# Batch 0 of a retention-plus-experts kernel, regrouped by token halves, with zero matmuls ahead and the remainder taken up later

## The chip, the cores and the metric

The kernel runs on one core of one Trainium2 chip. A core has TensorE (PE in the profile; its weight loads are PEld), VectorE (DVE), ScalarE (ACT), GpSimd (POOL) and SyncE (SP), each with its own instruction queue that is worked off in order, and 16 DMA engines that all queues share. The metric is the device time of one execution in microseconds (us); lower is better. Eight runs of the kernel before have a median of 561.19 us and lie between 557.19 and 563.51 us.

## The reference

Two layers follow one another. The first is a retention layer (attention with a decay per head and no softmax), the second mixes four small networks ("experts") with weights given per token.

```
q, k, v: [8 batches, 8 heads, 576 tokens, 64]
scores = q @ k.T / 8
ret    = scores * gamma[h] ** (i - j)      for i >= j, else 0      gamma[h] = 1 - 2 ** (-5 - h)
attn   = ret @ v                           -> x: [4608 tokens, 512]
p      = domain_probs / sum(domain_probs)  [4608, 4]
out    = sum over e of p[:, e] * (relu(x @ w1[e]) @ w2[e])     w1: [4, 512, 1024], w2: [4, 1024, 512]
```

## The kernel before

**Tokens and tiles.** The 4608 tokens are worked in 9 tiles of 512, `t = 0..8`. A batch has 576 tokens, so tile 0 is the first 512 tokens of batch 0, and tile 1 begins with the last 64 tokens of batch 0. `xt[t]` holds the attention output of a tile, transposed, as four blocks of 128 features (two heads each) by 512 tokens. The up projection multiplies it with `w1[e]` into PSUM, a relu writes it to `h`, and the down projection multiplies `h` with `w2[e]`.

**Attention in pieces.** The first 512 tokens of batches 0 and 1 are cut in four `Unit`s each, `(hf, g)`: the half `hf` of 256 tokens and the group `g` of four heads. For a unit, `cast` scales k by a decay table and turns k, q, v to bf16 (k on VectorE, q on ScalarE, v on GpSimd or ScalarE). A transposition of q and k follows: for batch 0 on TensorE (`trans_pe`, L477, with copies out of PSUM on ScalarE, L485, and on VectorE, L486), for batch 1 by a DMA on SP's queue (`trans_dma`, L488). `scores` multiplies k by q and VectorE masks the result (L508). `kv` makes the running key-value state, which ScalarE copies to `sbd` (L538). `values` adds both shares, and VectorE writes them to `xt` times the table `gq` (L570). Units of `hf = 1` also need the state of `hf = 0`. The last 64 tokens of a batch are the remainder, `Rem`: `cast` (L290, L293), two DMA transpositions into `kT` and `qT` (L299), `scores` (L305), `values` (L311, L313) for all heads at once.

**The start.** SP issues the loads of the four units of batch 0 (12 loads of 256 KB, L117), then those of the mixing weights. ScalarE makes the four tables `gq` (L157) before the first cast. Then the units run in the order (0,0), (1,0), (0,1), (1,1), as the loop at L587 writes them. GpSimd issues the weight loads in this order: `w1[0]` between two casts, `w2[0]`, `w1[1]`, `w2[1]`, `w1[2]`, the remainder of batch 0, `w2[2]`, unit 0 of batch 1, `w1[3]`, unit 1 of batch 1, `w2[3]`. Each weight load writes 1 MB as bf16 from fp32.

**Tile 0 and its slots.** For each of the four experts the loop at L691 issues four `up_group`s (8 matmuls of 512 columns each) and two `down_plain`s (16 matmuls of 512 columns each). After each of these six pieces `run(slots, n)` issues what was put into the slot of that number, so slot 6e+i is after up group i of expert e, and slots 6e+4 and 6e+5 are after the down pieces. The order of the instructions is written out by hand; each engine takes its own in this order. In the slots of tile 0 lie:

- the remainder of batch 0: `cast` and the DMA transpositions at 11, `scores` at 15, `values` at 16
- the four units of batch 1 (vs[0] to vs[3]): cast and DMA transpositions at 14, 17, 21, 24; scores and kv at 18, 21, 24, 28; values at 19, 22, 26, 30 (24 and more are slots of tile 1)
- four loads of the mixing weights of tile 1, `pB`, 256 KB each, on SP, at 17
- sums of w2 blocks on VectorE (`w_sum`) from 17 on

Tiles 1 to 8 follow with the same kind of slots. Their down projection uses seven products in place of eight.

**PSUM.** All matmul results go through a ring of four tiles of two banks (`ring_tile`), so a piece can only start when the reader of the piece four before it is done. In tile 0 the reader of an up piece is the relu on ScalarE (L330).

Of the kernel before, what the change touches and what calls it, by code (L numbers as in the profile page):

```python
# [9 lines left out]
FP32 = mybir.dt.float32  # L10
BF16 = mybir.dt.bfloat16
Copy = mybir.ActivationFunctionType.Copy
Exp = mybir.ActivationFunctionType.Exp
Relu = mybir.ActivationFunctionType.Relu
MULT = mybir.AluOpType.mult
# [8 lines left out]
def kernel(  # L24
# [10 lines left out]
    nc = tc.nc  # L35
    B, H, S, D = q.shape
    N, E = moe_domain_probs.shape
    _, Dm, F = moe_w1.shape
# [3 lines left out]
    NC = 4  # L42
    SM = NC * C
    R = S - SM
    NP = H // 2
    NDC = Dm // 128
    NFC = F // 128
    NT = 512
# [7 lines left out]
    const = ctx.enter_context(tc.tile_pool(name="const", bufs=1))  # L56
# [5 lines left out]
    tpool = ctx.enter_context(tc.tile_pool(name="tpool", bufs=1))  # L62
# [3 lines left out]
    def ring_tile(name, shape, dt=FP32):  # L66
        return ring.tile(shape, dt, tag="ring", name=name)
# [19 lines left out]
    rawr = {n: const.tile([128, NP, 2, D], FP32, name=f"rawr_{n}") for n, _ in srcs}  # L87
# [11 lines left out]
    def load_w1(e):  # L99
        return nc.gpsimd.dma_start(out=w1_sb[e], in_=moe_w1[e].rearrange("(dc p) f -> p dc f", p=128))  # L100
# [7 lines left out]
    epool = early.enter_context(tc.tile_pool(name="epool", bufs=1))  # L108


    NU = 4
# [6 lines left out]
                          in_=src[b, 4 * g:4 * g + 4, 2 * C * hf:2 * C * hf + 2 * C, :]  # L118
                          .rearrange("h (p r) d -> p h (r d)", r=2))

    units0 = ((0, 0), (1, 0), (0, 1), (1, 1))
    p0 = epool.tile([128, NT // 128, E], FP32, name="p0")
    prb = tpool.tile([128, N // 128, E], FP32, tag="p1", name="prb")
    for u, (hf, g) in enumerate(units0):
        load_unit({n: raw0[u][n][:, :, :, :].rearrange("p h r d -> p h (r d)") for n in "kqv"}, 0, hf, g, nc.sync)
    nc.sync.dma_start(out=p0, in_=moe_domain_probs[0:NT, :].rearrange("(g p) e -> p g e", p=128))
    nc.sync.dma_start(out=prb, in_=moe_domain_probs.rearrange("(p t) e -> p t e", p=128))


    pos_0 = epool.tile([128, 2, 2], FP32)  # L130
    nc.gpsimd.iota(pos_0, pattern=[[2 * C, 2], [1, 2]], base=0, channel_multiplier=2,
# [14 lines left out]
    for h in range(H):  # L146
        nc.vector.tensor_scalar_mul(gk0[:, :, h, :], pos_0, -lg[h])
    nc.scalar.activation(gk0, gk0, Exp)
    lgp = epool.tile([128, NP], FP32)
    for p in range(NP):  # L150
        nc.vector.memset(lgp[0:64, p:p + 1], lg[2 * p])
        nc.vector.memset(lgp[64:128, p:p + 1], lg[2 * p + 1])
    lsc = epool.tile([128, 1], FP32)
    nc.vector.memset(lsc, math.log(scale))
    gq = const.tile([128, NP, S], FP32)
    for p in range(NP):
        nc.scalar.activation(gq[:, p, :], pos_i, Exp, scale=lgp[:, p:p + 1], bias=lsc)  # L157

    tri = const.tile([128, C], BF16)
# [4 lines left out]
    def later_constants():  # L164
        nc.gpsimd.memset(tri, 1.0)
        nc.gpsimd.affine_select(out=tri, in_=tri, compare_op=mybir.AluOpType.is_ge, fill=0.0,
                                base=0, channel_multiplier=-1, pattern=[[1, C]])
        nc.gpsimd.tensor_copy(trir[0:R], tri[0:R, 0:R])
        nc.gpsimd.tensor_copy(trir[R:2 * R], tri[R:2 * R, R:2 * R])
        pos_j = epool.tile([128, NC + 1], FP32)  # L170
        nc.gpsimd.iota(pos_j[:, 0:NC], pattern=[[C, NC]], base=0, channel_multiplier=1,
                       allow_small_or_imprecise_dtypes=True)
        for j in range(2):
            nc.gpsimd.iota(pos_j[64 * j:64 * j + 64, NC:NC + 1], pattern=[[0, 1]], base=SM, channel_multiplier=1,
                           allow_small_or_imprecise_dtypes=True)
        for h in range(H):
            nc.vector.tensor_scalar_mul(gk[:, :, h], pos_j[:, 0:NC], -lg[h])
        nc.scalar.activation(gk, gk, Exp)
        nc.vector.tensor_scalar(gkr, lgp, pos_j[:, NC:NC + 1], -1.0, op0=MULT, op1=MULT)
        nc.scalar.activation(gkr, gkr, Exp)  # L180
        for n in "kqv":
            nc.gpsimd.memset(rawr[n], 0.0)


    NTT = N // 128
# [1 line left out]
    pn, psm = pns[:, 0:E, :], pns[:, E, :]  # L187
    pd = dpool.tile([E, N], FP32, name="pd")

    ps0 = epool.tile([128, NT // 128], FP32, name="ps0")  # L190
    pm0 = const.tile([128, NT // 128, E], FP32, name="pm0")

    def mixing_weights0():
        nc.vector.tensor_reduce(ps0, p0, axis=mybir.AxisListType.X, op=ADD)
        nc.vector.tensor_scalar_add(ps0, ps0, 1e-9)
        nc.vector.reciprocal(ps0, ps0)
        nc.vector.tensor_tensor(pm0, p0, ps0[:, :].unsqueeze(2).to_broadcast([128, NT // 128, E]), op=MULT)

    def mixing_weights():
        nc.vector.tensor_reduce(psm, prb, axis=mybir.AxisListType.X, op=ADD)  # L200
        nc.vector.tensor_scalar_add(psm, psm, 1e-9)
        nc.vector.reciprocal(psm, psm)
        nc.vector.tensor_tensor(pn, prb[:, :, :].rearrange("p t e -> p e t"),
                                psm.unsqueeze(1).to_broadcast([128, E, NTT]), op=MULT)
        nc.sync.dma_start(out=pd[:, :].rearrange("e (p t) -> p e t", p=128), in_=pn)

# [2 lines left out]
    def load_p(t, e, eng):  # L209
        pB[t, e] = ppool.tile([128, NT], FP32, tag="pB", name="pB")  # L210
        eng.dma_start(out=pB[t, e], in_=pd[e:e + 1, t * NT:(t + 1) * NT].to_broadcast([128, NT]))  # L211
# [108 lines left out]
    def up_group(h, t, e, i):  # L320
        ph = ring_tile("ph", [128, 2, NT])
        x = xt_of(t)
        for f in range(2):
            fc = 2 * i + f
            for dc in range(NDC):
                nc.tensor.matmul(ph[:, f, :], lhsT=w1_sb[e][:, dc, fc * 128:(fc + 1) * 128],  # L326
                                 rhs=x[:, dc, :], start=(dc == 0), stop=(dc == NDC - 1))
        fk = e * NFC + 2 * i
        if t == 0:
            nc.scalar.activation(h[:, fk:fk + 2, :], ph, Relu)  # L330
            return
        nc.vector.scalar_tensor_tensor(h[:, fk:fk + 2, :], ph, 0.0,  # L332
                                       pB[t, e][:, :].unsqueeze(1).to_broadcast([128, 2, NT]), op0=MAX, op1=MULT)
        if i == NFC // 2 - 1 and t + 1 < n_nt:
            load_p(t + 1, e, nc.gpsimd)

    def up_half(h, t, half, e, i):
        ph = ring_tile("ph", [128, 4, NT // 2])
        x = xt_of(t)
        c = slice(256 * half, 256 * half + 256)  # L340
        for f in range(4):
            fc = 4 * i + f
            for dc in range(NDC):
                nc.tensor.matmul(ph[:, f, :], lhsT=w1_sb[e][:, dc, fc * 128:(fc + 1) * 128],  # L344
                                 rhs=x[:, dc, c], start=(dc == 0), stop=(dc == NDC - 1))
        fk = e * NFC + 4 * i
        nc.vector.scalar_tensor_tensor(h[:, fk:fk + 4, c], ph, 0.0,  # L347
                                       pB[t, e][:, c].unsqueeze(1).to_broadcast([128, 4, NT // 2]), op0=MAX, op1=MULT)
        if half == 1 and i == 1:
            load_p(t + 1, e, nc.gpsimd)  # L350
# [230 lines left out]

    bfv0 = lambda g: {(n, hf): bf0[n][:, hf, g] for n in "kqv" for hf in range(2)}
    us = [Unit(0, hf, g, raw0[u], bfv0(g)) for u, (hf, g) in enumerate(units0)]
    us[0].cast(nc.gpsimd)
    us[0].trans_pe()
    us[1].cast(nc.gpsimd)
    for u in range(NU):  # L587
        us[u].scores()
        us[u].kv()
        if u + 1 < NU:  # L590
            us[u + 1].trans_pe()
        if u == 0:
            load_w1(0)
        if u + 2 < NU:
            us[u + 2].cast(nc.gpsimd)
        us[u].values()
    raw1u = {n: raw1[n][:, :, :, :].rearrange("p c j d -> p (c j d)") for n in "kqv"}
    raw1d = {n: raw1u[n].rearrange("p (h x) -> p h x", h=4) for n in "kqv"}
    raw1c = {n: raw1u[n].rearrange("p (h r d) -> p h r d", h=4, r=2) for n in "kqv"}
# [17 lines left out]
    load_w1(1)  # L617
    load_w2(1)
    load_w1(2)
    mixing_weights0()  # L620
    later_constants()
    mixing_weights()
    load_rem(0, nc.gpsimd)
    load_w2(2)
    load_v(0, nc.gpsimd)
# [3 lines left out]
    early.close()  # L629
    hp = ctx.enter_context(tc.tile_pool(name="hp", bufs=1))  # L630
    h = hp.tile([128, E * NFC, NT], BF16, name="h")


    def attention(slots, b, at):
# [13 lines left out]
    def remainder(slots, b, at):  # L648
        add = lambda i, f: slots.setdefault(i, []).append(f)
        x = Rem(b)  # L650
        l, c, s, o = at
        if b > 0:
            add(l, lambda: load_rem(b))
        add(c, x.cast)
        add(c, x.trans_dma)
        add(s, x.scores)
        add(o, x.values)
# [4 lines left out]

    slots = {}
    add = lambda i, f: slots.setdefault(i, []).append(f)
    remainder(slots, 0, (-1, 11, 15, 16))

    def v_cast(u):
        vs[u].cast()
# [9 lines left out]
        vs[u].scores()  # L678
        vs[u].kv()

    for u, (c, sc, o) in enumerate(((14, 18, 19), (17, 21, 22), (21, 24 + 0, 24 + 2), (24 + 0, 24 + 4, 24 + 6))):
        add(c, lambda u=u: v_cast(u))
        add(sc, lambda u=u: v_head(u))
        add(o, lambda u=u: vs[u].values())
    add(17, lambda: [load_p(1, e, nc.sync) for e in range(E)])
    for j in range(4):
        for wi, which in enumerate((3, 1, 2, 4)):
            add((17, 19, 22, 25)[j] + wi // 2, lambda which=which, j=j: w_sum(which, 4 * j, 4 * j + 4))
# [1 line left out]
    n = 0  # L690
    for e in range(E):  # L691
        for i in range(4):
            up_group(h, 0, e, i)
            run(slots, n)
            n += 1
        for m in range(2):
            down_plain(h, 0, e, m)
            run(slots, n)
            n += 1

    HK = KH // 2
    for t in range(1, n_nt):
        slots = {i - 24: f for i, f in slots.items() if i >= 24} if t == 1 else {}
# [19 lines left out]
        n = 0  # L723
# [43 lines left out]
```

## Time and profile before

| what | value |
|---|---|
| median of 8 runs | 561.19 us |
| the profiled execution's own time | 560.94 us |
| its span, first to last instruction | 559.2 us |
| PE busy | 535.1 us, 96% of the span |
| PEld busy | 351.5 us, 63% |
| DVE busy | 375.2 us, 67% |
| ACT busy | 110.5 us, 20% |
| POOL busy | 55.0 us, 10% |
| mean granted TensorE clock | 0.989 |
| DMA moved | 64.28 MB, 115 GB/s over the span |

The profile is of one execution. Its time of 560.94 us is 1.7 us more than its span, and 0.25 us below the median of the eight runs. Busy shares are means over the whole span. The slices of the page divide the span in 40 parts of 14.0 us each. Times such as "at 58.7" are microseconds from the first instruction. A matmul's busy time runs to its modelled end, and successive matmuls overlap, so the rate is read from the starts. A DMA's landing is counted from its issue. The DMA share is the mean over 16 engines and can exceed 1 where packets overlap.

### The profile page before, as it was taken

The numbers are of one execution on the slowest core, as the hardware profiler recorded it, in microseconds if no ns is written. First come the engines' busy times: TensorE is split into PE (matmuls) and PEld (weight loads), VectorE is DVE, ScalarE is ACT, GpSimd is POOL, SyncE is SP. The second block draws the span as 40 slices with busy tenths as digits, with TensorE's granted clock in tenths as the row PEclk, the third lists the DMA queues.
The fourth block names the chain that finished last, engine by engine and source line by source line (L and its number), as shares of the span: only waits on it lengthen the run. The fifth ranks groups of instructions, "written<-read, shape, count | busy, mean of one in ns | idle before, by whom it ended". The sixth has DMA issues, their size and how long they took to land.

```text
span 559.2 us, 10528 instructions
## 1 busy us (share of the span) xinstructions
PE 535.1 (96%) x4388; PEld 351.5 (63%) x4416; DVE 375.2 (67%) x550; ACT 110.5 (20%) x216; POOL 55.0 (10%) x95
## 2 busy tenths in 40 slices
PE   4999399999999999999999999999999999999996
PEld 3544145888854686468745874488447854884485
DVE  4622057988668974898389838984788567736871
ACT  5433312303221120222013211131113100000010
POOL 4614101000000000000000000000000000000000
PEclk9999799999999999999999999999999999999999
DMA  8999918547744862578146724653367131010010
GB/s 236 204 209 251 163 29 215 114 89 155 157 111 115 148 155 66 127 128 173 57 104 142 150 83 95 153 132 104 90 131 148 54 94 42 21 57 19 1 39 38
DMA packets 147454, 64.28 MB, mean 115 GB/s; under 512 B 127216, under 2 KB 137584, under 8 KB 147408
## 3 DMA queue, kind: packets, MB, share of 16 engines
q1 hardware_dynamic: 137760, 44.35, 35.6%
q0 software_dynamic: 9648, 19.27, 16.0%
q8 instruction: 34, 0.56, 0.4%
q14 instruction: 12, 0.10, 0.1%
HBM read 53.56 MB, written 9.51 MB: 113 GB/s over the span
## 4 chain that ended last, share of the span: by engine, by line
PE 91%; DMA 4%; DVE 2%; ACT 1%; issue 1%; SPq 1%; POOL 0%; POOLq 0%; ACTq 0%
PE ph L326 36%; PE pd L429 35%; PE po L359 5%; PE ph L344 5%; DMA qTr<-bfr_q 3%; PE kvp L246 2%; PE o L270 1%; PE s L259 1%; PE o L273 1%; PE kvp L525 1%; DMA rawr_q<-in_q_dram 1%; PE s L506 1%; PE pt L483 1%; ACT gq L157 1%; SPq L82 0%
## 5 line engine op out<-in xcount | busy, mean ns | idle before, releaser
L326 PE MATMUL ph<-xt,w 128*128 128x512 bf16 x1000 | 225.8, 380 | 1.4 <-DVE xt L570 0.2
L326 PEld LDWEIGHTS <-w 128*128 128x128 bf16 x1024 | 99.0, 98 | 114.4 <-issue 1.1
L332 DVE SCALAR_TENSOR_TENSOR h<-ph,pB 128x1024 bf16<-128x1024 f32 x112 | 136.3, 1222 | 31.9 <-PE ph L326 31.6
L429 PEld LDWEIGHTS <-h 128*128 128x128 bf16 x1024 | 98.8, 98 | 12.2
L429 PEld LDWEIGHTS <-s 128*128 128x128 bf16 x768 | 74.3, 98 | 8.9
L429 PE MATMUL pd<-wx,h 128*128 128x256 bf16 x512 | 61.2, 273 | 0.0
L429 PE MATMUL pd<-wx,s 128*128 128x256 bf16 x512 | 61.1, 273 | 0.0
L251 ACT ACTIVATE sbd<-kvp 64x256 bf16<-64x256 f32 x48 | 18.1, 378 | 112.2 <-PE kvp L246 111.9
L261 DVE TENSOR_TENSOR sT<-s,tri 128x1024 bf16<-128x1024 f32 x24 | 29.2, 1216 | 11.2 <-PE s L259 11.2
L211 POOL DMA_DIRECT2D pB<-pd x28 | 15.2, 542 | 206.2 <-DVE h L332 159.2
L455 POOL TENSOR_TENSOR ob<-v,p 128x256 f32<-128x256 f32 x16 | 11.6, 723 | 231.7 <-DVE v L452 139.4
L359 PE MATMUL po<-wx,h 128*128 128x512 bf16 x124 | 30.7, 401 | 0.2
L429 PE MATMUL pd<-t4w,h 128*128 128x256 bf16 x256 | 30.6, 273 | 0.0
L429 PE MATMUL pd<-t2w,s 128*128 128x256 bf16 x256 | 30.6, 273 | 0.0
L429 PE MATMUL pd<-t3w,h 128*128 128x256 bf16 x256 | 30.6, 273 | 0.0
L446 DVE TENSOR_TENSOR u<-pd,p 128x256 f32<-128x256 f32 x16 | 6.8, 422 | 35.4 <-issue 29.5
L344 PE MATMUL ph<-xt,w 128*128 128x256 bf16 x256 | 29.2, 273 | 0.2 <-DVE h L347 0.2
L280 DVE TENSOR_TENSOR xt<-o,gq 128x384 bf16<-128x384 f32 (+6 forms) x48 | 18.0, 416 | 16.4 <-PE o L273 16.4
L344 PEld LDWEIGHTS <-w 128*128 128x128 bf16 x256 | 24.6, 98 | 3.3 <-issue 0.2
L437 ACT ACTIVATE p<-pd 128x256 f32<-128x256 f32 x16 | 6.1, 384 | 96.4 <-PE pd L429 74.7
L330 ACT ACTIVATE h<-ph 128x1024 bf16<-128x1024 f32 x16 | 16.4, 1022 | 41.5 <-PE ph L326 39.7
L408 DVE TENSOR_TENSOR h<-h 128x1024 bf16<-128x1024 bf16 x32 | 23.4, 770 | 0.0
(130 smaller groups left out, 418.3 us busy)
## 6 DMA issues: line engine op xcount, KB each, us to landing
pB<-pd POOLq DMA_DIRECT2D x28, 256.0 KB, 3.6
raw_k<-in_k_dram SPq DMA_DIRECT2D x48, 128.0 KB, 2.9
raw_q<-in_q_dram SPq DMA_DIRECT2D x48, 128.0 KB, 3.5
raw_v<-in_v_dram SPq DMA_DIRECT2D x48, 128.0 KB, 3.5
w<-in_moe_w_dram POOLq DMA_DIRECT2D x4, 1024.0 KB, 13.5
wx<-in_moe_w_dram POOLq DMA_DIRECT2D x4, 1024.0 KB, 16.8
out_dram<-oa SPq DMA_DIRECT2D x16, 256.0 KB, 2.1
out_dram<-ob SPq DMA_DIRECT2D x16, 256.0 KB, 2.0
```

The costliest lines, as they stand in the source:

```text
L211: eng.dma_start(out=pB[t, e], in_=pd[e:e + 1, t * NT:(t + 1) * NT].to_broadcast([128, NT]))
L251: nc.scalar.activation(sbd[r, self.p, :, r], kvp[r, :, :], Copy)
L261: nc.vector.tensor_tensor(self.sT[:, :, :, :].rearrange("p j c t -> p (j c) t"), s[:, :, :, :].rearrange("p j c t -> p (j c) t"), tri[:, : ...
L280: nc.vector.tensor_tensor(xt_of(t)[:, p, n0 + a - t * NT:n0 + z - t * NT], o[:, a:z], gq[:, p, a:z], op=MULT)
L326: nc.tensor.matmul(ph[:, f, :], lhsT=w1_sb[e][:, dc, fc * 128:(fc + 1) * 128], rhs=x[:, dc, :], start=(dc == 0), stop=(dc == NDC - 1))
L330: nc.scalar.activation(h[:, fk:fk + 2, :], ph, Relu)
L332: nc.vector.scalar_tensor_tensor(h[:, fk:fk + 2, :], ph, 0.0, pB[t, e][:, :].unsqueeze(1).to_broadcast([128, 2, NT]), op0=MAX, op1=MULT)
L344: nc.tensor.matmul(ph[:, f, :], lhsT=w1_sb[e][:, dc, fc * 128:(fc + 1) * 128], rhs=x[:, dc, c], start=(dc == 0), stop=(dc == NDC - 1))
L359: nc.tensor.matmul(po[:, g, :], lhsT=h[:, e * NFC + fc, ns * 128:(ns + 1) * 128], rhs=wx[e // 2][:, (e % 2) * NFC + fc, :, :].rearrange("p ...
L408: nc.vector.tensor_tensor(h[:, l, self.b], h[:, l, self.a], h[:, l, self.b], op=SUB)
L429: mm = nc.tensor.matmul(dst, lhsT=src[:, kk, tok], rhs=rhs(c), start=(start and c == 0), stop=(c == KH - 1), skip_group_check=True)
L455: nc.gpsimd.tensor_tensor(self.ob[:, HF:Dm], self.v, self.p5, op=ADD)
```

## The change

The units of batch 0 run in the order (0,0), (0,1), (1,0), (1,1): first all heads of tokens 0 to 255, then all heads of tokens 256 to 511. The up projection of expert 0 is done in token halves (`up_half`: 16 matmuls of 256 columns). Its two pieces for tokens 0 to 255 are issued ahead of `values` of the third unit and ahead of `values` of the fourth; the two for tokens 256 to 511 take the place of up groups 2 and 3 of the loop, and nothing is issued for up groups 0 and 1. For tile 0, `up_half` ends with the relu on ScalarE.

Eight matmuls of a zero tile are issued before the first transposition, and three after it. ScalarE makes two `gq` tables during the first unit and two during the second, no longer ahead of the first cast. The mixing weights and two decay tables are computed after the last unit. Some small tiles change their pool.

In the slots, the remainder's cast and transpositions move from 11 to 12, its scores from 15 to 18 and its values from 16 to 19. Unit 0 of batch 1 has scores and kv at 19 in place of 18, and values at 20 in place of 19. The four `pB` loads go from 17 to 15.

```diff
-    units0 = ((0, 0), (1, 0), (0, 1), (1, 1))
+    units0 = ((0, 0), (0, 1), (1, 0), (1, 1))
...
+    zz = epool.tile([128, 512], BF16)
+    nc.vector.memset(zz, 0.0)
+
+    def warm(n):
+        w = ring_tile("w", [128, 512])
+        for _ in range(n):
+            nc.tensor.matmul(w, lhsT=zz[:, 0:128], rhs=zz, start=True, stop=True)
...
-    for p in range(NP):
+
+    def make_gq(p):
         nc.scalar.activation(gq[:, p, :], pos_i, Exp, scale=lgp[:, p:p + 1], bias=lsc)
...
         fk = e * NFC + 4 * i
+        if t == 0:
+            nc.scalar.activation(h[:, fk:fk + 4, c], ph, Relu)
+            return
...
+    warm(8)
     us[0].cast(nc.gpsimd)
     us[0].trans_pe()
+    warm(3)
     us[1].cast(nc.gpsimd)
-    for u in range(NU):
+    for u in range(2):
         us[u].scores()
         us[u].kv()
-        if u + 1 < NU:
-            us[u + 1].trans_pe()
+        us[u + 1].trans_pe()
         if u == 0:
+            make_gq(0)
+            make_gq(1)
             load_w1(0)
-        if u + 2 < NU:
-            us[u + 2].cast(nc.gpsimd)
+            us[2].cast(nc.gpsimd)
+        else:
+            make_gq(2)
+            make_gq(3)
+            us[3].cast(nc.gpsimd)
         us[u].values()
+    us[2].scores()
+    us[2].kv()
+    us[3].trans_pe()
...
-    mixing_weights0()
-    later_constants()
-    mixing_weights()
+    pos_j = later_constants()
...
     h = hp.tile([128, E * NFC, NT], BF16, name="h")
+    up_half(h, 0, 0, 0, 0)
+    us[2].values()
+    us[3].scores()
+    us[3].kv()
+    up_half(h, 0, 0, 0, 1)
+    us[3].values()
+    mixing_weights0()
+    later_tables(pos_j)
+    mixing_weights()
...
-    remainder(slots, 0, (-1, 11, 15, 16))
+    remainder(slots, 0, (-1, 12, 18, 19))
...
-    for u, (c, sc, o) in enumerate(((14, 18, 19), (17, 21, 22), (21, 24 + 0, 24 + 2), (24 + 0, 24 + 4, 24 + 6))):
+    for u, (c, sc, o) in enumerate(((14, 19, 20), (17, 21, 22), (21, 24 + 0, 24 + 2), (24 + 0, 24 + 4, 24 + 6))):
...
-    add(17, lambda: [load_p(1, e, nc.sync) for e in range(E)])
+    add(15, lambda: [load_p(1, e, nc.sync) for e in range(E)])
...
-            up_group(h, 0, e, i)
+            if e > 0:
+                up_group(h, 0, e, i)
+            elif i > 1:
+                up_half(h, 0, 1, 0, i - 2)
             run(slots, n)
```

More of the change, by code (lines that the diff above doesn't have):

```diff
@@ L119, in load_unit @@
                           .rearrange("h (p r) d -> p h (r d)", r=2))
-    units0 = ((0, 0), (1, 0), (0, 1), (1, 1))
-    p0 = epool.tile([128, NT // 128, E], FP32, name="p0")
-    prb = tpool.tile([128, N // 128, E], FP32, tag="p1", name="prb")
+    units0 = ((0, 0), (0, 1), (1, 0), (1, 1))
+    pr_ = tpool.tile([128, N // 128 + NT // 128 + 1, E], FP32, tag="p1", name="pr_")
+    prb, p0, ps0 = pr_[:, 0:N // 128], pr_[:, N // 128:N // 128 + NT // 128], pr_[:, N // 128 + NT // 128]
     for u, (hf, g) in enumerate(units0):
@@ L148 @@
     nc.scalar.activation(gk0, gk0, Exp)
-    lgp = epool.tile([128, NP], FP32)
+    lgp = const.tile([128, NP], FP32)
     for p in range(NP):
@@ L169, in later_constants @@
         nc.gpsimd.tensor_copy(trir[R:2 * R], tri[R:2 * R, R:2 * R])
-        pos_j = epool.tile([128, NC + 1], FP32)
+        pos_j = const.tile([128, NC + 1], FP32)
         nc.gpsimd.iota(pos_j[:, 0:NC], pattern=[[C, NC]], base=0, channel_multiplier=1,
@@ L175, in later_constants, with later_tables @@
                            allow_small_or_imprecise_dtypes=True)
+        for n in "kqv":
+            nc.gpsimd.memset(rawr[n], 0.0)
+        return pos_j
+    def later_tables(pos_j):
         for h in range(H):
@@ L180, in later_constants @@
         nc.scalar.activation(gkr, gkr, Exp)
-        for n in "kqv":
-            nc.gpsimd.memset(rawr[n], 0.0)
     NTT = N // 128
@@ L188 @@
     pd = dpool.tile([E, N], FP32, name="pd")
-    ps0 = epool.tile([128, NT // 128], FP32, name="ps0")
     pm0 = const.tile([128, NT // 128, E], FP32, name="pm0")
@@ L196, in mixing_weights0 @@
         nc.vector.reciprocal(ps0, ps0)
-        nc.vector.tensor_tensor(pm0, p0, ps0[:, :].unsqueeze(2).to_broadcast([128, NT // 128, E]), op=MULT)
+        nc.vector.tensor_tensor(pm0, p0, ps0.unsqueeze(2).to_broadcast([128, NT // 128, E]), op=MULT)
     def mixing_weights():
@@ L202, in mixing_weights @@
         nc.vector.reciprocal(psm, psm)
-        nc.vector.tensor_tensor(pn, prb[:, :, :].rearrange("p t e -> p e t"),
+        nc.vector.tensor_tensor(pn, prb.rearrange("p t e -> p e t"),
                                 psm.unsqueeze(1).to_broadcast([128, E, NTT]), op=MULT)
```

## The prediction

> **What bounds the kernel now.** I read the slices first. Columns are 14 us each; PE's digit is its busy share in tenths, PEclk the granted clock, DMA the busy share of the 16 engines.
>
> ```profile
> PE   4999399999999999999999999999999999999996
> PEclk9999799999999999999999999999999999999999
> DMA  8999918547744862578146724653367131010010
> ```
>
> TensorE is full except in the first slice and in the fifth (55.9 to 69.9 us), and right after that its clock is down. The DMA engines are full from the start to the end of the fifth slice. From 90 us on nothing but TensorE sets the time, so an edit before it pays what it makes TensorE reach that point earlier. The change has two places, the start and the hole. Second view, TensorE's own waits (total, times, longest):
>
> ```profile
> PE sr L305 <- DMA qTr<-bfr_q: 9.7, 2, 9.1
> PE pt L483 <- DVE bf_k L469: 4.8, 1, 4.8
> PE s L506 <- DVE qkT L486: 1.6, 3, 1.1
> ```
>
> The hole is one wait of 9.1 us: the scores of the remainder for its DMA transposition. Third view, the stretches of time around it (busy us of PE, PEld, DVE, ACT, POOL, then PEclk, DMA share, GB/s):
>
> ```profile
> 58.60:62.00 3.40, 0.10 (x1) 0.00 (x0) 0.00 (x0) 2.42 (x4) 1.49 (x2) 1.00 1.21 208
> 62.00:65.00 3.00, 0.00 (x0) 0.00 (x0) 0.00 (x0) 0.00 (x0) 0.00 (x0) 0.57 1.38 189
> 65.00:67.80 2.80, 0.00 (x0) 0.00 (x0) 0.00 (x0) 0.00 (x0) 0.00 (x0) 0.50 1.28 115
> 70.00:75.00 5.00, 5.00 (x25) 2.10 (x24) 1.02 (x2) 0.00 (x0) 0.00 (x0) 0.73 0.06 19
> ```
>
> TensorE stands from 58.7 to 67.84, its clock halves within it, and it restarts slow. Price of the slow restart: the 16 weight loads of the down piece go from 67.98 to 73.56 there, 5.58 us; the same piece at full clock goes from 87.16 to 90.72, 3.56 us. So the hole costs 9.1 + 2.0 = 11.1 us. Fourth view, the DMA issues, asked for one stretch at a time (last number: us from issue to landing):
>
> ```profile
> w<-in_moe_w_dram POOLq DMA_DIRECT2D x1, 1024.0 KB, 9.8
> ```
> ```profile
> qTr<-bfr_q SPq DMA_TRANSPOSE x1, 12.4
> qkT<-bf_k SPq DMA_TRANSPOSE x1, 13.8
> ```
> ```profile
> qkT<-bf_q SPq DMA_TRANSPOSE x1, 13.5
> ```
>
> w1[0], issued at 10.11, lands at 19.9. The remainder's qTr, issued at 55.29, lands at 67.7; unit 0 of batch 1 behind it in the same queue, issued at 56.57 and 58.58, lands at 70.4 and 72.1. A transposition issued at 79.74, with the engines idle, took 2.4. Here they stand behind the weight and unit loads that have filled the engines since 2 us.
>
> **The hole, part by part.** The remainder's scores go from slot 15 to slot 18, so TensorE first does down pieces 0 and 1 of expert 2 and up group 0 of expert 3: 3.56 x 2 + 1.80 (one up group, from 82.61 to 86.21 for two) = 8.92 us. That brings it there at 58.7 + 8.92 = 67.6, less G, which is what the start gains. Their inputs are in: w1[3] landed at 55.7, needed at 65.8. The price of moving the cast from 11 to 12 is near nothing: its VectorE half waits, as before, only for the accumulation of slot 11 (bfr_k at 53.16; no VectorE work lies in slots 12 to 14), so kTr is issued at the same time; its ScalarE half comes after the relu of slot 12 (54.6), is done at 55.2, and qTr was issued at 55.29 anyway. The next relu is pushed by 0.5 us, which the PSUM ring hides: four pieces of 1.8 us against a relu of 1.02. So qTr lands at about 67.7 again, and the wait of 9.1 shrinks to about 0.2.
>
> What is late next is unit 0 of batch 1, now at slot 19. TensorE is there at 67.84 + 0.14 (scores of the remainder) + 1.80 (up group 1) + 0.42 (its values, 73.56 to 73.98) = 70.2. Its q lands at 72.1, so it waits 2.0 us, too short for the clock to fall (the row 58.60:62.00 holds 1.00 through 3.4 us of standing). From there to down piece 0 of expert 3: scores and kv 0.95 (79.28 to 80.23), two up groups 3.60, values 0.42, scores and kv of unit 1 0.95: 5.92. Start at 72.1 + 0.14 + 5.92 = 78.16. Before, it started at 87.16: a gain of **9.0 us**. In general, with L for that landing, 81.1 - L. If nothing were late it would be 11.3 + G.
>
> Where on the DMA queue does L come from? The pB loads move from slot 17 to 15: on SP's queue they pass unit 1's transpositions and come directly behind unit 0's, at about 60.2 instead of 82.3. They wait for nothing (pd landed at 34.5) and hold up nothing on SP: the next, unit 1, needs VectorE's accumulation of slot 17 and is issued at about 68; it lands behind pB and is needed at slot 21, near 77. The cost of pB: between 80 and 90 us, where they run before, the engines have shares of 0.46 and 0.44, 5 x 0.90 = 4.5 us, transpositions of unit 1 included. Behind unit 0 in the same queue they delay it by nothing; wholly ahead they would put L at 76.6. I take nothing, as they are issued later.
>
> [...] The rows show 12.4 to 13.8. I take the rows: L = 72.1.
>
> **The start (G).** The first down piece starts at 30.91 before. w1[0] keeps its place: GpSimd issues it after the same cast, whose input lands at the same time, so it lands at 19.9. TensorE takes its work in order and comes to the first up half earlier than that: before, the fourth unit's transpositions ended at 18.6; now the first q cast no longer stands behind the gq tables (it ran at 5.84, its data landed at 4.8: 1.0 us), and at full clock the units are shorter (scores of 16 matmuls 0.64 us here, 0.42 at 79.28). It arrives near 17 and waits about 3 us. The gq tables do not vanish: 0.78 each on ScalarE, two in unit 0 and two in unit 1, ahead of the next cast, and VectorE's xt waits for them; this takes back about what the earlier cast gives, which also goes into that wait. After 19.9: four up halves, 64 matmuls at 0.109 (64 in 7.15 us from 111.64) = 7.0; values of units 2 and 3 2 x 0.53 (101.50 to 102.03), scores and kv of unit 3 1.42 (96.48 to 97.90); then the wait for xt, 0.65 as before (23.34 to 23.98): 30.1, and some 0.4 for kv waiting for a ring tile whose relu is only done at about 22.9. So 30.5: **G = +0.4 us**. Half matmuls against whole ones cost nothing: 32 of 512 took 6.9. The 11 zero matmuls lie before 7.3 us, 8 x 0.43 = 3.4 us from about 1.3, in the idle 4.8 us ahead of the first transposition; without that cover they would cost 3.4. Mixing weights and tables (2.3 us on VectorE before) now follow unit 3's xt; their first reader is the accumulation at 34.6.
>
> [...] The 9s of PEclk at the very start are not to be trusted, as matmuls of 512 columns start every 0.43 us until 24.8, twice the later spacing. [...] If instead the clock is at half at 20, the first up half costs 16 x 0.105 = 1.7 us more and values 0.3: G = -1.6. By the row alone (3.4 us of rest before the fall) I take +0.4 and keep -1.6 for the range.
>
> **The sum.** G matters little: the gain is fixed by L, which the DMA backlog sets. TensorE would still be early at slot 19 with G = -1.6 (71.8). Only the issue of unit 0's transposition, which follows its relu, shifts with G. So 560.94 - 9.0 = 551.9 on the profiled execution; the median of the runs lies 0.25 above it: **552.2 us**. Its own range, L within 1.4 us: 550.8 to 553.6.
>
> **The rivals.** [...]
> (2) *They land late*: half clock in the start issues them 1.6 later, or pB slows them by up to its 4.5. L between 73.7 and 76.6, gain 4.5 to 7.4: 553.8 to 556.7. For it: these queues are full; against it: pB is behind.
> (3) *The wait only moves*, as the backlog stretches with the queue: within 0.5%, which is 2.8 us and about what this measurement can tell from no change. That needs L above 78.3, 6 us later than before.
> (4) *Slower*: the transposition of unit 0 is starved at slot 19. Once the wait there is over 3.4 us (L above 73.7) the clock falls and the restart adds 2.0, so the gain is 79.1 - L, and it decides from L = 81.9 on, 9.8 us later than before. The place is right, but the known additions are 1.6 and 4.5 us; together 6.1, at L = 78.2, a gain of 0.9.
>
> **How the numbers follow.** The likeliest case 0.46, (1) 0.20, (2) 0.26, (3) 0.04, (4) 0.04. Faster 0.92, same 0.04, slower 0.04. The range runs from just under (1) to near the end of (2), 549.0 to 556.4, and leaves out (3), (4) and a little of (2): about 1 to 2 in 10.
>
> **What would show it.** In the changed profile: no wait of TensorE over 3.4 us after 20; the wait for qTr under 1 us, and one of about 2 us for unit 0's qkT; full clock through the fifth slice; first down piece at 30.5 (32.5 if the clock was half); down piece 0 of expert 3 at about 78. Wrong would be: landings after 76, or a start that loses more than 3 us, as when w1[0] lands after 22.

## The result and the profile after

The changed kernel takes 550.99 us (median of 11 runs) against 560.33 us for the kernel before (31 runs). The ratio is 0.9839 with a 95% interval of 0.9817 to 0.9861, so it saves 9.0 us (7.8 to 10.3). The ratio leaves out the one long execution of 559.9 us. The forecast was 552.2 us and 9.0 us saved.

Nine of the eleven executions lie between 550.2 and 551.9 us, one took 555.2, and one took 559.9. The first profile is of this last one. So a second profile of the same kernel (experiment 1, span 550.0 us) stands for the usual case, and the long one is kept as a case of its own. First the slices of the usual one, 13.75 us each:

```profile
PE   7799999999999999999999999999999999999996
PEclk9599999999999999999999999999999999999999
DMA  9999926377547633574256715762475131110011
```

The hole in the fifth slice is gone, and with it the slow clock after it. The DMA engines are full for five slices, as before. New is the 5 of PEclk in the second slice. TensorE's waits in the same profile:

```profile
PE ph L355 <- DMA w<-in_moe_w_dram: 2.9, 1, 2.9
PE w L136 <- DVE zz L131: 1.3, 1, 1.3
PE s L520 <- DVE qkT L500: 1.2, 2, 0.8
PE o L561 <- DVE sT L522: 0.7, 1, 0.7
PE pt L497 <- ACT bf_q L485: 0.6, 2, 0.4
```

No wait for a DMA transposition is left at all. The one large wait is at the start, for w1[0] (L355 is the matmul of `up_half`). The stretches that were empty before are full here (columns as in the prediction):

```profile
58.60:62.00 3.40, 3.40 (x18) 1.54 (x16) 0.00 (x0) 2.92 (x5) 0.41 (x1) 1.00 1.31 168
62.00:65.00 3.00, 2.96 (x15) 1.17 (x14) 0.00 (x0) 1.76 (x3) 1.07 (x2) 1.00 1.04 156
65.00:67.80 2.80, 2.80 (x15) 1.27 (x14) 1.41 (x2) 0.00 (x0) 0.00 (x0) 1.00 1.08 300
```

Next come the transpositions that the prediction turned on, with the time from issue to landing at the end of each line. The remainder's qT was issued at 58.0 and unit 0's q at 61.3.

```profile
qTr<-bfr_q SPq DMA_TRANSPOSE x1, 7.0
qkT<-bf_q SPq DMA_TRANSPOSE x1, 5.6
```

They landed at 65.0 and 66.9, in about half of the 12.4 and 13.5 us of before, and TensorE only came for them at 69.9 and 72.6. In the long execution the same two, issued at 57.9 and 61.2, took this:

```profile
qTr<-bfr_q SPq DMA_TRANSPOSE x1, 11.9
qkT<-bf_q SPq DMA_TRANSPOSE x1, 16.2
```

and TensorE's longest wait there is the one that the prediction placed at slot 19:

```profile
PE s L520 <- DMA qkT<-bf_q: 4.9, 1, 4.9
PE ph L355 <- DMA w<-in_moe_w_dram: 2.7, 1, 2.7
```

Two marks on TensorE's queue carry the sum. The first down piece of expert 0 starts at 30.7 before (weight load) and at 33.55 in the usual execution after; down piece 0 of expert 3 starts at 87.16 before and at 78.67 after. So between these two executions the start loses 2.85 us, the stretch with the hole gives 11.3, and the point behind it comes 8.5 us earlier. The rest of the span is 472.0 us before and 471.3 after.

### The profile page after: what moved, and what is told of

It reads as the page before. It is cut to its first block, busy times and chain, and to the rows that moved or that the text cites. A ratio compares the mean times of both kernels' runs of the same rounds, so it can differ in the third digit from the quotient of the medians.

```text
span 558.0 us, 10615 instructions
## 1 busy us (share of the span) xinstructions
PE 539.2 (97%) x4432; PEld 355.1 (64%) x4459; DVE 375.4 (67%) x551; ACT 110.3 (20%) x216; POOL 55.0 (10%) x95
## 3 DMA queue, kind: packets, MB, share of 16 engines
q0 software_dynamic: 9648, 19.27, 16.2%
## 4 chain that ended last, share of the span: by engine, by line
PE 92%; DMA 6%; issue 0%; DVE 0%; SPq 0%; ACT 0%; POOLq 0%; POOL 0%; DVEq 0%
PE ph L337 38%; PE pd L443 35%; PE ph L355 7%; PE po L373 4%; DMA qkT<-bf_q 3%; DMA w<-in_moe_w_dram 2%; PE kvp L257 2%; PE o L281 1%; PE s L270 1%; PE o L284 1%; DMA raw_1v<-in_v_dram 1%; PE kvp L539 1%; PE o L561 0%; SPq L117 0%; PE o L568 0%
## 5 line engine op out<-in xcount | busy, mean ns | idle before, releaser
L337 PE MATMUL ph<-xt,w 128*128 128x512 bf16 x968 | 220.3, 381 | 1.4 <-issue 0.2
L337 PEld LDWEIGHTS <-w 128*128 128x128 bf16 x992 | 96.0, 98 | 111.3 <-issue 2.2
L443 PE MATMUL pd<-wx,h 128*128 128x256 bf16 x512 | 61.2, 273 | 0.0
L355 PE MATMUL ph<-xt,w 128*128 128x256 bf16 x320 | 38.7, 280 | 3.4 <-DMA w<-in_moe_w_dram 2.7
L355 PEld LDWEIGHTS <-w 128*128 128x128 bf16 x320 | 31.4, 100 | 8.6 <-DMA w<-in_moe_w_dram 3.0
L272 DVE TENSOR_TENSOR sT<-s,tri 128x1024 bf16<-128x1024 f32 x24 | 29.2, 1216 | 11.3 <-PE s L270 11.3
L222 POOL DMA_DIRECT2D pB<-pd x28 | 15.2, 542 | 205.8 <-DVE h L343 158.7
L373 PE MATMUL po<-wx,h 128*128 128x512 bf16 x125 | 28.5, 379 | 0.2
L383 DVE SCALAR_TENSOR_TENSOR acc<-po,pm,acc 128x512 f32<-128x512 f32 x12 | 8.5, 747 | 24.0 <-PE po L373 24.0
```

The lines of the kernel that those rows point to most:

```text
L272: nc.vector.tensor_tensor(self.sT[:, :, :, :].rearrange("p j c t -> p (j c) t"), s[:, :, :, :].rearrange("p j c t -> p (j c) t"), tri[:, : ...
L373: nc.tensor.matmul(po[:, g, :], lhsT=h[:, e * NFC + fc, ns * 128:(ns + 1) * 128], rhs=wx[e // 2][:, (e % 2) * NFC + fc, :, :].rearrange("p ...
L443: mm = nc.tensor.matmul(dst, lhsT=src[:, kk, tok], rhs=rhs(c), start=(start and c == 0), stop=(c == KH - 1), skip_group_check=True)
```

## The experiments

Theory A: the four DMA transpositions stand behind the stream of weight loads, and when the last of the four, unit 0's q, lands (L) decides what is saved. Rival B: the new start carries a part. Rival J came up after the first batch: the loads of unit 2, in flight beside the transpositions, jam them.

### 1. The changed kernel again

No edit.

> The changed kernel, unaltered, for a second profile: the one at hand is of its longest execution (559.88 us), in which unit 0's q landed at 77.4. Theory A (the DMA backlog sets the gain through that landing, L): L between 70 and 73.5, TensorE waits 0 to 3 us for it, full clock after it, down piece 0 of expert 3 at L + 6.1, time 550 to 552 us. Rival B (the start has gained and the landing is no bound): no wait at slot 19, the first down piece clearly before 30.9.

552.4 us (four runs, 550.3 to 555.1), a ratio of 0.987 to the kernel before, with its 95% interval in brackets [0.983, 0.992]. L was 66.9, earlier than theory A had it, TensorE did not wait, and the first down piece was later than before. So neither expectation fits whole: the landing was no bound in the profiled execution, and the start had not gained but lost.

### 2. The slots alone

```diff
-    remainder(slots, 0, (-1, 11, 15, 16))
+    remainder(slots, 0, (-1, 12, 18, 19))
...
-    for u, (c, sc, o) in enumerate(((14, 18, 19), ...
+    for u, (c, sc, o) in enumerate(((14, 19, 20), ...
...
-    add(17, lambda: [load_p(1, e, nc.sync) for e in range(E)])
+    add(15, lambda: [load_p(1, e, nc.sync) for e in range(E)])
```

> The kernel before with the new slots alone (remainder 12, 18, 19; unit 0 of batch 1 at 19 and 20; pB at 15), the old start. Theory A: all of the gain is here, 9 us, 550.5 to 552.5 us, and TensorE waits about 2 us at slot 19. Rival B: part of the gain belongs to the start, and this gives 5 us or less, 555 or more.

551.8 us, ratio 0.988 [0.985, 0.991]. Its waits in the whole span:

```profile
PE pt L483 <- DVE bf_k L469: 4.7, 1, 4.7
PE s L506 <- DVE qkT L486: 1.4, 2, 1.1
PE pt L483 <- ACT bf_q L471: 1.2, 1, 1.2
PE sr L305 <- DMA qTr<-bfr_q: 0.7, 1, 0.7
```

The large wait for qT is gone with the old start; the 0.7 us in the last line is for the remainder of a later batch. Within what can be told, all of the saving is in the slot numbers.

### 3. The start alone

The changed kernel with the three slot lines of experiment 2 put back.

> The changed kernel with the old slots (remainder 11, 15, 16; unit 0 at 18 and 19; pB at 17): the new start alone. Theory A: what the start gains or loses is swallowed by the wait at slot 15, whose end the backlog sets: 559 to 562 us, no difference from before beyond 0.3%. Rival B: 2 us or more faster, 558 or less. Rival C (the start loses, since the clock falls in it): 562 to 565, if the transpositions also come later.

558.2 us, ratio 0.999 [0.996, 1.002]. No difference, as theory A expects. In its profile, of a long execution, the wait for qT is 9.8 us, and it ends when the transposition lands (57.42 + 13.1 = 70.5), whatever the start did.

### 4. No zero matmuls

The changed kernel without the two lines `warm(8)` and `warm(3)`.

> The changed kernel without its 11 zero matmuls. Theory A: the first up half waits for w1[0] (about 20) with or without them, and the landing of unit 0's q hides a start that is up to 2 us later: 550.5 to 552.5 us, the same as the changed kernel. Rival B (the zero matmuls carry a gain): 1.5 us or more slower than the changed kernel, 552.5 or more.

552.1 us, ratio 0.986 [0.983, 0.990], the same as the changed kernel. But not for the reason given: the first down piece starts at 31.84, earlier than with the zeros (33.55), and TensorE does not wait for the qT of batch 0 (landed at 66.3, taken up at 68.4). It waits 0.4 us for unit 0's q, which landed at 71.3, and 0.4 us for unit 1's. What the zeros do to the clock is shown with experiment 10.

### 5. The loads of unit 2 at slot 16

```diff
-        if u == 0:
-            load_v(2, nc.gpsimd)
-        elif u == 2:
+        if u == 2:
...
+    add(16, lambda: load_v(2, nc.gpsimd))
```

> The kernel before, where only the loads of unit 2 of batch 1 (768 KB on GpSimd's queue) are issued at slot 16 in place of slot 14, so that they are not in flight with the four DMA transpositions. Theory J (these loads and the transpositions jam each other): the remainder's qT lands within 3 us of w2[3], about 64 to 66, TensorE's wait at slot 15 is 4 to 6 us in place of 9, 555 to 557.5 us. Theory A (the whole backlog sets the landing): qT lands near 67 again, the wait is 8 us or more, 559 to 561.5 us.

559.35 us, ratio 0.999 [0.997, 1.001]. This run tells nothing about theory J, because the edit did nothing: the loads were issued at 55.3, 59.4 and 60.1, among the transpositions (55.8, 57.1 and 59.1) as before (54.7, 58.8 and 59.6). Between slots 14 and 16 GpSimd has nothing else to do, so it ran ahead to them at once and was only held by their buffers (6.3 us until the cast of k, 3.4 until that of q). So here the slot number moved them by 0.6 us at most; in experiment 6 it moves a load by 11.9, as loads in front of it in GpSimd's queue wait.

### 6. w2[3] behind the transpositions

```diff
     load_v(1, nc.gpsimd)
-    load_w2(3)
...
+    add(15, lambda: load_w2(3))
```

This is the kernel before in all else. On GpSimd's queue w2[3] now stands behind the loads of unit 2, which wait for casts of slot 14, so it is issued at 60.9 in place of 49.0.

> The kernel before, where only the load of w2[3] (1 MB) goes from the start of GpSimd's list to slot 15, behind the loads of unit 2. Theory A (the transpositions stand behind the weight stream): they find the engines nearly free at 54 to 60 and land in 3 to 6 us, the wait at slot 15 is under 3 us, 549 to 553 us. Theory J (the unit loads jam them): landings of 8 us or more and a wait over 5 us, 555 or more.

550.7 us, ratio 0.984 [0.981, 0.986]: this one edit saves what the whole change saves. The transpositions, issued at 55.8 and 59.1, now take

```profile
qTr<-bfr_q SPq DMA_TRANSPOSE x1, 3.5
```
```profile
qkT<-bf_q SPq DMA_TRANSPOSE x1, 4.3
```

and TensorE waits 0.2 us at slot 15, the old place. The loads of unit 2 were in flight beside them (issued at 55.3, 59.4, 60.1) and landed in about 4 us as well. So theory J fails as a cause by itself; whether these loads add to the delay once w2[3] stands in front is not tested. The stretch that was the hole, with a DMA share of 0.58 to 0.99 (the last columns are clock, share, GB/s):

```profile
55.00:58.60 3.60, 3.60 (x18) 1.66 (x17) 0.00 (x1) 2.19 (x4) 0.75 (x1) 1.00 0.99 187
58.60:62.00 3.40, 3.23 (x20) 1.40 (x18) 0.42 (x1) 2.98 (x5) 2.39 (x3) 1.00 0.58 109
```

w2[3] lands at 71.3 and is first needed near 76. So the cause of the hole is shown: a 1 MB load was placed ahead of transpositions that were due some 17 us before it (59.4 against 76.4).

But much of the delay comes after that load has landed. Before, w2[3] landed at 64.7 and unit 0's q 7.4 us later. In the row 65.00:67.80 of the prediction the engines are busy (share 1.28) and move 115 GB/s. In experiment 1, just after w2[3] landed (62.7), transpositions and loads of unit 2 were in flight too, and the engines moved twice as much:

```profile
63.00:66.00 3.00, 3.00 (x15) 1.37 (x14) 0.85 (x2) 0.76 (x2) 0.07 (x1) 1.00 1.07 230
```

Read for all executions in the 2.8 us from the landing of w2[3] on, it was 206 and 242 GB/s in experiments 1 and 2, 172 in experiment 7, and 83 to 135 in the others with a late q (before, the long one, experiments 3, 4, 5 and 8). So the load in front starts the delay, and in some executions what stands behind it then moves at about half the rate. Why only in some is not shown.

### 7. w1[0] one cast earlier

```diff
     warm(3)
+    load_w1(0)
     us[1].cast(nc.gpsimd)
...
             make_gq(1)
-            load_w1(0)
```

> The changed kernel with the load of w1[0] issued one cast earlier on GpSimd's queue (about 7.5 in place of 10). If the first up half waits for w1[0] alone, it lands at 17 to 18.5 and the first down piece starts 2 us earlier than in the changed kernel; with no wait left at slots 18 and 19 this goes through: 548.5 to 550 us. If the bytes of the unit loads in front of it count (they share the engines), it lands at about 20 again, or the later units come later, and the time is 550.5 to 552.5.

555.1 us, ratio 0.992 [0.989, 0.994]: some 4 us slower than the changed kernel, beyond the worse of the two expectations. w1[0], issued at 6.9, took 11.5 us and landed at 18.4, but the loads of unit 3, issued after it, came late (raw_3q took 11.1 and landed at 19.3, and a TensorE transposition waited 3.3 us for unit 3). GpSimd's cast of unit 3 then ran at 20.2, and the weight loads behind it on that queue began at 20.7 in place of 15.2. The whole stream was late: w2[3] landed at 70.8, L was 74.0, and TensorE waited 2.4 us at slot 19. The clock fell there too:

```profile
71.80:74.10 2.30, 0.00 (x0) 0.00 (x0) 1.15 (x3) 0.45 (x1) 0.00 (x0) 1.00 0.93 175
75.20:78.50 3.30, 3.30 (x8) 0.95 (x8) 1.95 (x3) 0.76 (x2) 0.00 (x0) 0.50 0.63 179
```

The start of the same chain is in the long execution of the changed kernel without any edit: there unit 3's v took 8.6 us to land, GpSimd waited for it (5.36 us in the first line), and w2[0] was issued at 18.7:

```profile
18.12 0.61 POOL L489 CAST bf_v<-raw_3v 128x512 bf16<-128x512 f32 x1 [5.36 <-DMA raw_3v<-in_v_dram]
18.68 0.92 POOL L103 DMA_DIRECT2D wx<-in_moe_w_dram  x1
```

### 8. pB at slot 17

The changed kernel with `add(17, ...)` for the four pB loads.

> The changed kernel with the four pB loads back at slot 17, behind unit 1's transpositions. The prediction's reading (they lie behind unit 0's transpositions in the same queue and cost nothing): 550.5 to 552.5 us, the same as the changed kernel. Rival (they slow the transpositions): unit 0's q lands earlier and the time is 1 to 4 us less in runs that wait at slot 19.

551.6 us, ratio 0.986 [0.983, 0.989], as the changed kernel. In the profile, of the longest of its four executions (554.3 us), L was 73.4 although pB was only issued at 71.2, so pB is not what makes the transposition late. This execution also shows what a wait of 3 us at slot 19 costs (stretches around it):

```profile
70.40:73.60 3.20, 0.25 (x8) 0.15 (x6) 1.43 (x3) 0.72 (x1) 0.00 (x0) 1.00 1.43 126
73.60:78.00 4.40, 4.40 (x52) 2.15 (x56) 2.52 (x3) 0.80 (x3) 0.00 (x0) 0.61 0.75 237
```

The clock fell here after 3.0 us of standing, and the trace's clock record has it at half for 3.4 us.

### 9 to 12. w2[3] late, with three starts, beside the old kernel with w2[3] late

All four have w2[3] at slot 15 as in experiment 6. Experiment 9 is the changed kernel with it; 11 is the same without the two `warm` lines; 12 is the kernel of experiment 6 again; 10 adds to 9

```diff
+    warm(6)
     up_half(h, 0, 0, 0, 0)
```

In the clock records of two traces, of the kernel before and of the long execution, the complete stretches of full and of half clock last whole multiples of 3.41 us: 37.55 and 10.24 before, 6.83, 13.65, 51.20 and 6.83 in the long execution. By windows the expectation of experiment 10 means such steps.

> The changed kernel with the load of w2[3] at slot 15, behind the loads of unit 2, as in the run before that did this to the old kernel. If w2[3] ahead of the transpositions is the whole cause of late landings, unit 0's q lands within 6 us of its issue, no wait over 0.5 us at slots 18 and 19, no long executions, 549.5 to 551 us. If other loads do it too, the spread of 550 to 560 stays.

> The same with six more zero matmuls directly ahead of the first up half, where TensorE waits 2 to 3 us for w1[0]. If the half clock there comes from too little work in the windows before, the clock is full again by about 21 to 23, the first down piece starts 1 to 2 us earlier and the time is 0.5 to 2 us under the run without them. If the clock needs a whole window of dense work after 20 anyway, or the zeros end after w1[0] has landed, no difference or up to 1 us more.

> The same without any zero matmul. Nothing later hides a start that is slower, so this shows what the eleven zeros are worth. If the clock that they raise falls again after 7 us of the short matmuls of the units, they are worth nothing: within 0.7 us of the run with them, either way. If they help: 1.5 us or more slower than with them.

> The old kernel with w2[3] at slot 15 again, for a comparison on one chip: 550 to 551.5 us. The three changed kernels beside it differ from it by the start and the slots alone. If the new start is worth anything, they are 1 us or more below it; if not, within 0.7 us of it.

| run | median us (range of 6) | first down piece | down piece 0 of expert 3 |
|---|---|---|---|
| 9, eleven zeros | 551.13 (550.30 to 552.08) | 32.26 | 77.45 |
| 10, seventeen zeros | 550.64 (550.00 to 554.87) | 30.34 | 75.77 |
| 11, no zeros | 551.72 (550.94 to 553.29) | 32.08 | 78.83 |
| 12, old start and slots | 550.94 (549.93 to 557.18) | 31.86 | 76.89 |

The last two columns are when these pieces start in the one profiled execution of each run. The times can't be told apart (the intervals of all four overlap), so the new start is worth nothing that this measurement shows, and no version beats the changed kernel beyond it. Experiment 9's transpositions landed within 4 us, as expected, and its range has no long execution. Those of 10 and 12 each have one (554.9 and 557.2), so moving w2[3] does not rule them out. In experiment 11 unit 3's v was late and w2[0] was issued at 18.9. The weight loads behind it came late too (w1[3] landed at 58.9), unit 0's q took 6.6 us, and TensorE still waited 1.6 us. So w2[3] is not the only load that can make the transpositions late.

The clock tells what the zeros do. Experiment 1 (eleven zeros, all before 7.3 us):

```profile
4.00:8.00 4.00, 3.56 (x46) 1.88 (x43) 1.37 (x3) 1.23 (x2) 1.85 (x2) 1.00 1.10 288
8.00:12.00 4.00, 2.63 (x65) 1.81 (x64) 2.91 (x6) 3.51 (x7) 1.46 (x2) 1.00 1.19 289
12.00:16.00 4.00, 3.10 (x58) 1.99 (x55) 3.63 (x7) 3.67 (x7) 2.06 (x3) 0.60 1.21 237
16.00:20.00 4.00, 1.58 (x20) 1.14 (x16) 1.20 (x2) 1.35 (x3) 3.68 (x11) 0.50 1.20 193
20.00:24.00 4.00, 3.48 (x16) 2.24 (x16) 0.00 (x0) 0.00 (x0) 3.94 (x8) 0.50 1.21 194
24.00:28.00 4.00, 4.00 (x70) 2.92 (x70) 1.89 (x3) 1.78 (x3) 0.76 (x2) 0.69 1.14 217
```

and experiment 10 (six more, issued in the wait for w1[0]):

```profile
16.00:20.00 4.00, 2.60 (x15) 1.41 (x14) 0.49 (x2) 1.28 (x3) 3.62 (x11) 0.77 1.23 209
20.00:24.00 4.00, 4.00 (x78) 3.03 (x77) 1.49 (x3) 1.09 (x2) 3.67 (x7) 1.00 1.22 208
```

In experiment 1 the clock is full when the units begin, and falls at about 13 although TensorE was 66% busy with their short matmuls from 8 to 12. It is at half through the first up half, which takes 3.6 us in experiments 1 and 9 and 1.9 in experiment 10. With the six zeros ahead of it the full clock is back by 18 (24.8 in experiment 9), and the first down piece comes 1.9 us earlier than in experiment 9. Of these 1.9 us, 1.7 are still there at down piece 0 of expert 3, but the spans differ by 0.6 only (549.7 and 549.1): experiment 10 has a wait of 0.9 us for a later remainder that experiment 9 has not.

## Why the prediction was right, and where it was not

**The hole.** That moving the scores to slot 18 would take the wait of 9.1 us and the slow restart away, and cost the start of nothing else, was right: experiment 2 has it with nothing but slot numbers, and experiment 3 shows that the start alone saves nothing. "If nothing were late it would be 11.3 + G": in experiment 1 nothing was late, the start gave -2.85, and 11.3 - 2.85 = 8.45 against the 8.49 between the marks.

**The rows.** The step that failed is "I take the rows: L = 72.1". L was 66.9 in the usual execution of the changed kernel and 65.8 in experiment 2, and in neither did TensorE wait for a transposition at slots 18 and 19. That is case (1) of the chances, early landings, to which 0.20 was given. Its gain of 11.3 + 0.4 us (549.5 us), from which the range begins, was the author's estimate: no run shows the 0.4, the runs showed a start that loses, 2.85 us in experiment 1. The row was one execution, and L is not one value: it was 77.4 in the long execution. Unit 0's q against the landing of w2[3], over the profiles:

| run | q issued | w2[3] landed | q landed | q took |
|---|---|---|---|---|
| 1, changed | 61.3 | 62.7 | 66.9 | 5.6 |
| 2, slots alone | 59.7 | 62.9 | 65.8 | 6.1 |
| 5, loads at slot 16 | 59.1 | 63.1 | 70.4 | 11.2 |
| 4, no zeros | 59.6 | 63.7 | 71.3 | 11.7 |
| 8, pB at 17 | 59.2 | 63.9 | 73.4 | 14.2 |
| before | 58.6 | 64.7 | 72.1 | 13.5 |
| 3, start alone | 60.7 | 66.2 | 75.6 | 14.9 |
| changed, long execution | 61.2 | 67.0 | 77.4 | 16.2 |
| 7, w1[0] early | 60.4 | 70.8 | 74.0 | 13.7 |
| 6, w2[3] late | 59.1 | 71.3, issued 60.9 | 63.4 | 4.3 |

With w2[3] issued behind it, unit 0's q takes 3.9 to 4.4 us (experiments 6, 9, 10 and 12; 6.6 in experiment 11, where w1[3] was late); with w2[3] in front, about 6 or 11 to 16. That it stands in front is the shown cause. Why it costs 6 in one execution and 14 in another with nearly equal times of issue (experiments 2 and 8) stays open.

**The start.** "G = +0.4" failed: it was -2.85 between the two profiles, beyond the -1.6 that was kept for the range. Each of these marks is one draw as well: the first down piece starts between 30.7 and 31.9 in the five profiles with the old start, and between 31.5 and 33.6 in the five with eleven zeros and w1[0] in its place. The means differ by 1.4 us, near the -1.6. The wait for w1[0] came as described (2.9 us, expected about 3), and its landing nearly so (20.5, expected 19.9). What failed is "by the row alone (3.4 us of rest before the fall) I take +0.4". The row tells how the clock fell while TensorE stood still (1.00 in 58.60:62.00, 0.57 in 62.00:65.00); in the start it fell, at about 13 in experiment 1, though TensorE was 66% busy from 8 to 12. That it would be full at 20 was the author's estimate; all six profiles with eleven zeros have PEclk at 5 or 6 in the second slice, from about 14 to 28 us. The term left out is the first up half and the unit behind it at half clock; the clock is full again only from about 26.5. From the first up half to the second it is 6.5 us in experiment 1 and 3.9 in experiment 10 at full clock: 2.6 us, where the case of -1.6 had 1.7 + 0.3, without the scores and kv of unit 3.

**Why the number held all the same.** The two misses have opposite signs: in experiment 1 the early landing gave 2.3 us more than the sum of 9.0 had, and the start, which a sum fixed by L holds at nothing, took 2.85. That they nearly cancel is luck. The forecast of 9.0 us is right in size, but not by its likeliest case.

**G matters little.** This held where the transpositions are late (experiment 3), and failed where they are early: then each microsecond of the start counts at slot 18.

**pB, the casts.** Both costed at nothing, both right: experiment 8 for pB; in experiment 1 kTr is issued right after its cast at 55.9 to 56.6, and qTr 1.4 us later, as before.

**The clock at slot 19.** "Too short for the clock to fall" was said of a wait of 2.0 us, with 3.4 us as the measure. There is less room: the clock did not fall after 1.6 us in experiment 11, but it did after 2.4 in experiment 7 and 3.0 in experiment 8, and in the long execution of the changed kernel the wait of 4.9 us was followed by 0.50 from 80 to 84. That is rival (4)'s mechanism. From the landing to down piece 0 of expert 3 the prediction has 6.06 us; it was 7.6 in experiment 8, 7.8 in 7 and 9.1 in the long execution, so the restart cost some 1.5 to 3.0 where the sum had 2.0. Rivals (2) and (3) leave this cost out, although their L lies above the 73.7 from which (4) counts it: by the prediction's own 2.0, (2) gains 2.5 to 5.4 us in place of 4.5 to 7.4, and (3) begins at L = 76.3.

## What to carry to other kernels

Where a wait ends on a small DMA that was issued long before, look at what stands in front of it on the shared engines and when that load is due. Here, moving one 1 MB load that was due later saved as much as giving the wait 9 us of other work to cover it. A landing time read from one execution is one draw, and so is a mark on TensorE's queue: look at the same place in a second profile before a sum rests on it. As to matmuls that only raise the clock: eleven of them ahead of a stretch of short ones did not last here (full clock for 6.8 us, then half). Six directly ahead of the dense work brought a mark forward by 1.9 us in one pair of profiles (experiments 9 and 10), and no time that could be told.

## What the runs showed of the hardware that was not expected

In all seven profiles of kernels with zero matmuls ahead, the trace's clock record gives full clock for 6.8 us and then half clock for 6.8, 10.2 or 13.7 us, two, three or four steps of 3.41. In the long execution it is full from 5.65 to 12.48 us and half to 26.13. Each time the fall comes within the units: in the two steps before it TensorE was 60% to 79% busy (73% and 69% in the long execution), with no gap as long as 0.8 us. So standing still, as at slot 15 before, is not the only thing that the clock fell after.

On the DMA engines, a transposition of one unit, 2.4 us alone, took 4.3 us beside unit loads (experiment 6), and up to 16.2 us with a 1 MB weight load in front (the long execution). In that execution one unit's load, issued at 9.5, landed late (8.6 us in place of 5.1). Through a cast on GpSimd's queue this shifted the weight loads behind it by about 3 us, and some 60 us later TensorE waited 4.9 us at slot 19. That the late load is what made this execution long is read from one trace, not tested; experiment 7 shows the same chain, set off by an edit.
